# Attention beside a Fourier transform: bursts of six key chunks across the borders of units

## The chip, the cores and the metric

The kernel runs on one core of a Trainium2 chip. The metric is the device time of one execution in microseconds (us). A core has TensorE for matmuls (PE in the rows; PEld are its weight loads), VectorE (DVE), ScalarE (ACT), GpSimd (POOL) and SyncE (SP, which here issues nearly all transfers). Matmuls accumulate in PSUM, eight banks of 128 x 512 fp32; only TensorE, VectorE and ScalarE reach it. Each engine runs its own instructions in order, and waits for other engines at semaphores.

## The reference

Two independent halves, whose outputs stand side by side in `out` (2048 x 2048, fp32).

```
x (2048 x 1024), 32 heads of 32, one key head and one value head for all:
  q = x wq; k = x wk; v = x wv
  p = softmax(q k^T / sqrt(32)) over the 2048 keys, for each head
  out[:, :1024]  = concat_heads(p v) wo
x' (2048 x 1024), Fourier mixing:
  a = x' Dre^T; b = x' Dim^T            (1024 x 1024 matrices)
  out[:, 1024:] = Sre a - Sim b          (2048 x 2048 matrices)
```

## The kernel before, in words

**Two kinds of work share TensorE.** All dense products (the projection to q, the Fourier half, the product with `wo`) are *fills*. A fill is one 128 x 128 by 128 x 512 matmul in fp32r; three of them (high part by high part, high by low, low by high) make one product with more precision. They come in groups, each of which accumulates in one bank `psb` and is then emptied: 32 groups of 24 fills (q), 112 of 12 and 112 of 24 (Fourier, by two schemes of seven products in place of eight), 24 of 24 (`wo`), and at the very end the last eight groups for `wo`. There are two banks `psb` (`ps_b`, line 123).

**Attention runs in steps.** A *unit* is four heads by 512 queries: 32 units, each of 32 steps, 1024 steps in all (the loop over `n` at the end of the kernel). Step `n` belongs to unit `n // 32`. It does these things, in this order:

- `score_step(n + 44)` works 44 steps ahead, on the softmax's row maxima and sums. `scores` makes 128 queries by 1024 keys in a tile `pss` (two matmuls; `ps_s`, line 121, has two such tiles of two banks), VectorE reduces the maximum, and one step later `row_sums` lets ScalarE take the exponentials' sum in the same tile. After a unit's last scores, `lse_1` to `lse_4` combine the sums: small operations on VectorE and ScalarE, and on TensorE one transposition into `psb` (`lse_3`, at n mod 32 = 24). With its own `aside` this stands ahead of the step's scores.
- One function of the list `ends` is run, if there is one.
- `expo` makes the scores once more, transposed (128 keys by two heads of 512 queries, tile `pst`, two matmuls; `ps_t`, line 122, has one such tile), and ScalarE writes the exponentials `p`. Two steps make a *chunk* of 128 keys; a unit has 16 chunks. There are 13 tiles `p` (line 586).
- At n mod 32 = 16 `inverse` loads the unit's reciprocal sums, spread over partitions, to the one tile `rb`.
- At n mod 32 = 0, 12 and 22 comes a *burst*, `pv` (line 686): fp32 matmuls of the values with the waiting chunks `p`, four heads side by side in the array's columns. The three bursts of a unit take 6, 5 and 5 chunks (`CUT`), the third one at step 0 of the next unit. A burst accumulates in a bank `psb`; VectorE copies the first into `ov` and adds the others. After the third, three functions go to `ends`, one for each of the next three steps: GpSimd multiplies `ov` by `rb`, rounds it into `oh`, and takes the rest into `ol`; `store` then sends both to memory over SP.
- `level(n)` deals out fills with `take`, except in a burst step. `goal(n)` is the number of fills due at step `n`, linear in `n`. Up to the next burst, `level` takes in each step the rounded-up share of what is missing to the goal at that burst, so that a stretch of steps between two bursts has its longer steps first.

**`aside`** (line 368) runs ahead of each burst and each transposition. If the open group has had fewer than six of its fills, or has fewer than six left, it takes fills up to that point, so that the other bank `psb` has been emptied, or the group is closed. What it takes is missing from what `level` deals out later.

**What sets the order.** Every engine's instructions are issued in the order in which the program states them (`Ordered`, line 58). Which of a pool's buffers a tile gets is decided when the program is built: a tile takes a buffer whose former tile has been released by its last reader, and waits for that reader on the chip. Loads, splits into high and low parts and stores of the fills are issued ahead of their use by a number of fills (`Line`).

The lines that the change touches are `CUT` and `pv`, `ENDS` and `level`, the burst in the loop over `n`, and the last burst behind it.

Of the kernel before, what the change touches and what calls it, by code (L numbers as in the profile page):

```python
# [8 lines left out]
F32 = mybir.dt.float32  # L9
F32R = mybir.dt.float32r  # L10
# [6 lines left out]
P = 128  # L17
# [3 lines left out]
DH = 32  # L21
W = 512
NG = 8
NQ = 4
NC = 16
# [62 lines left out]
def tile_kernel(ctx: ExitStack, tc, xT, wq, wkv, wo, xbT, wT, cT, out):  # L88
    nc = tc.nc
    te = Ordered(tc, nc.tensor)  # L90
    act = Ordered(tc, nc.scalar)
    dve = Ordered(tc, nc.vector)
    gp = Ordered(tc, nc.gpsimd)
# [3 lines left out]
    def pool(stack, name, bufs, **kw):  # L97
        kw.setdefault("reuse_waits", "tile")
        return stack.enter_context(tc.tile_pool(name=name, bufs=bufs, **kw))
# [4 lines left out]
    oh_d = [dram.tile([NG, P, W], F32, name=f"oh_{b}") for b in range(NQ)]  # L104
    ol_d = [dram.tile([NG, P, W], F32, name=f"ol_{b}") for b in range(NQ)]
# [10 lines left out]
    v = keep.tile([P, NC, DH], F32, name="v")  # L116
# [4 lines left out]
    ps_s = pool(ctx, "ps_s", 2, space=PSUM)  # L121
# [12 lines left out]
    def move(q, to, of):  # L134
        q.dma_start(to.bitcast(F32), of.bitcast(F32))
# [117 lines left out]
    def add(gs):  # L253

        for g in gs:
            i0 = g.at = end[0]
            end[0] += g.n
            if groups and g.set[0] is not groups[-1].set[0]:
                prev["set"] = prev["this"]
                prev["this"] = i0  # L260
            for c, it in enumerate(g.right):
                if it.need is None:
                    it.need = i0 + 3 * c
                    p0 = prev["set"]
                    it.due = min(it.need, p0 + (i0 - p0) * (g.first + c + 1) // (len(g.set) * len(g.right)))
                    RL.items.append(it)
                it.last = i0 + 3 * c + 2
            for c, it in enumerate(g.left):
                if it.need is None:
                    it.need = it.due = i0 + 12 * c  # L270
                    ML.items.append(it)
                it.last = i0 + 12 * c + 11
            for it in g.ys:
                it.due = i0 + g.n
                ylist.append(it)
            groups.append(g)
# [24 lines left out]
    def soon(f):  # L301

        if pos["fill"] <= START:
            f()
        else:
            at(pos["fill"] + BEHIND, f)

    def store(to, of, key=None):
        def go():
            move(sp, to, of)  # L310
            if key:
                ready.add(key)
        soon(go)

    cur = {"at": 0, "bank": None, "group": 0}
    used = [0, 0]

    def bank(name, open_=False):

        b = 1 - cur["bank"] if cur["bank"] is not None else int(used[1] < used[0])  # L320
        cur["at"] += 1
        used[b] = cur["at"]
        if open_:
            cur["bank"] = b
        return ps_b[b].tile([P, W], F32, name=name)
# [16 lines left out]
    def take(n):  # L342
        for _ in range(n):
            if cur["group"] >= len(groups):
                return
            g = groups[cur["group"]]
            j = pos["fill"] - g.at
            if j == 0:
                cur["ps"] = bank("psb", True)
            if j % 3 == 0:  # L350
                RL.force(g.right[j // 3])
            if j % 12 == 0:
                ML.force(g.left[j // 12])
            product(g, cur["ps"], j)
            pos["fill"] += 1
            if j == g.n - 1:
                cur["group"] += 1
                assert all(hasattr(it, "done") for it in g.ys)
                g.post(cur["ps"])
                cur["at"] += 1  # L360
                used[cur["bank"]] = cur["at"]
                cur["bank"] = None
                if g.ys:
                    at(pos["fill"] + 2 * BEHIND, lambda n=len(g.ys): yused.__setitem__(0, yused[0] + n))
            pump()
            run_later()

    def aside():

        if cur["group"] >= len(groups):  # L370
            return
        g = groups[cur["group"]]
        j = pos["fill"] - g.at
        if 0 < j < 6:
            take(6 - j)
        elif j > g.n - 6:
            take(g.n - j)
# [33 lines left out]
    def q_group(b, g, xs):  # L411
        left = [Item([(lambda q=q: wq[g, :, q * 4:(q + 1) * 4, :], 1)]) for q in range(2)]

        def post(ps):
            qh = op.tile([P, W], F32R, name="qh")
            ql = yp.tile([P, W], F32, name="y0").bitcast(F32R)
            if pos["fill"] <= START:
                act.activation(qh, ps, AF.Copy, scale=scale)
            else:
                dve.tensor_scalar_mul(qh, ps, scale)  # L420
            dve.scalar_tensor_tensor(ql, ps, scale, qh.bitcast(F32), op0=ALU.mult, op1=ALU.subtract)
            store(qh_d[b][g], qh)
            store(ql_d[b][g], ql, ("q", b, g))
        return Group(left, xs, post)
# [104 lines left out]
    def wo_set(e):  # L529
        return [Item([(lambda g=g: wo[g * P:(g + 1) * P, e * W:(e + 1) * W], 1)]) for g in range(NG)]  # L530
# [45 lines left out]
    start = [q_group(0, g, sets[0]) for g in range(2)]  # L576
# [12 lines left out]
    onp = pool(ctx, "onp", 1)  # L589

    units = [(b, g) for b in range(NQ) for g in range(NG)]
    SU = 32
    LEAD = 12
    total = SU * len(units)
    qst, nm, lse, pt, ov, rb, pend = ({} for _ in range(7))
    ends = []
# [84 lines left out]
            te.matmul(ps[:, a], kst[:, c * P:(c + 1) * P], qst[u][:, 2 * hp_ + a], start=True, stop=True)  # L681
        act.activation(pt[u, c, hp_], ps, AF.Exp)

    CUT = (0, 6, 11, NC)

    def pv(u, k):

        aside()
        ps = bank("psb")
        for c in range(CUT[k], CUT[k + 1]):  # L690
            for h in range(4):
                te.matmul(ps[h * DH:(h + 1) * DH], v[:, c], pt[u, c, h // 2][:, h % 2], start=c == CUT[k], stop=c == CUT[k + 1] - 1)
        if k == 0:
            ov[u] = onp.tile([P, W], F32, name="ov")
            dve.tensor_copy(ov[u], ps)
        else:
            dve.tensor_add(ov[u], ov[u], ps)
        cur["at"] += 1
        if k == len(CUT) - 2:
            b, g = units[u]  # L700
            hi_ = onp.tile([P, W], F32R, name="oh")
            lo_ = onp.tile([P, W], F32R, name="ol")
            lse["out"] = hi_, lo_

            last = u + 1 == len(units)
            e = dve if last else gp

            def low():
                e.tensor_sub(lo_, ov[u], hi_.bitcast(F32))
                if not last:  # L710
                    store(oh_d[b][g], hi_)
                    store(ol_d[b][g], lo_, ("o", b, g))

            ends.append(lambda: e.tensor_mul(ov[u], ov[u], rb[u]))
            ends.append(lambda: e.tensor_copy(hi_, ov[u]))
            ends.append(low)

    def score_step(s):

        if s < total:  # L720
            u, r = divmod(s, SU)
            if r == SU - 6 and u + 1 < len(units):
                open_unit(u + 1)
        if SU <= s < SU * (len(units) + 1) and s % SU == TURN:
            lse_3((s - SU) // SU)
        if s < total:
            scores(s)
        row_sums(s - 1)
        u, e = divmod(s - SU, SU)
        if 0 <= u < len(units):  # L730
            for f in LSE.get(e, ()):
                f(u)
# [52 lines left out]
    def goal(n):  # L785
        return PRO + (FILL - PRO - LAST - MORE * (total - QUIET)) * n // total + MORE * max(n - QUIET, 0)


    ENDS = [2 * c for c in CUT]

    def level(n):
        r = n % SU
        if r in ENDS:
            return
        more = min(e for e in ENDS if e > r) - r
        left = goal(n + more) - pos["fill"]
        take(left - left * (more - 1) // more)

    for n in range(total):
        u, r = divmod(n, SU)  # L800
        if n == total - 12:
            w1 = wo_set(1)
            add([o_group(NQ - 1, t, e, ws) for e, ws in ((0, w0), (1, w1)) for t in range(4)])
        score_step(n + SU + LEAD)
        if ends:
            ends.pop(0)()
        expo(n)
        if r == 16:
            inverse(u)
        if r in ENDS and n:  # L810
            pv((n - 1) // SU, (ENDS.index(r) - 1) % (len(CUT) - 1))
        level(n)


    last = groups[len(groups) - 8:]
    take(last[0].at - pos["fill"] - 12)
    pv(len(units) - 1, len(CUT) - 2)
    while ends:
        ends.pop(0)()
    hi7, lo7 = lse["out"]  # L820
# [27 lines left out]
    for t, g in enumerate(last[4:]):  # L848
        ps = whole(4 + t)
# [41 lines left out]
```

## Time and profile before

| what | us |
|---|---|
| median of 3 runs (lowest, highest) | 2753.52 (2752.26, 2755.05) |
| the profiled execution | 2752.88 |
| its span, first to last instruction | 2750.8 |
| TensorE busy | 2742.4 |
| ScalarE busy | 2165.2 |
| GpSimd busy | 1596.6 |
| VectorE busy | 1579.5 |

The granted clock of TensorE is 1.000 over the whole span. A row of a timeline gives the start in us from the span's start, the duration, engine, operation, output<-input and the count of instructions merged in the row; in brackets the idle time before it. A row of the groups gives the count, busy us and mean ns of one, then idle time before. A row of the waits gives us in total, times, and the longest. An fp32 matmul stands as two records, an fp32r matmul as one. Every line of the program shows as one and the same line of a helper, so groups are told apart by their tiles' names: `psb<-p,v` are the bursts, `psb<-rh,mh` and its two companions the fills, `pss<-kst,qst` the scores, `pst<-qst,kst` the transposed scores.

### The profile page before, as it was taken

What the parts mean: (1) busy time and instruction counts of PE and PEld (TensorE: products, weight loads), DVE (VectorE), ACT (ScalarE), POOL (GpSimd) and SP (SyncE); (2) the same over time, 40 slices, a digit from 0 to 9 for tenths busy, and PEclk for the clock granted to TensorE, in tenths of its full rate; (3) what the DMA queues carried; (4) which work ended last, traced back from release to release, by engine and by line L of the source; (5) the groups of instructions that cost most, each with busy time, mean ns of one, the idle gap of its engine ahead of it and who ended that gap; (6) DMA issues with size and microseconds to landing.
All of it is one profiled execution on the core that took longest, in us unless ns stands there. A gap on an engine that the chain in (4) does not pass through costs nothing.

```text
span 2750.8 us, 40206 instructions
## 1 busy us (share of the span) xinstructions
PE 2742.4 (100%) x13868; PEld 1928.3 (70%) x13868; DVE 1579.5 (57%) x1798; ACT 2165.2 (79%) x3131; POOL 1596.6 (58%) x1591
## 2 busy tenths in 40 slices
PE   9999999999999999999999999999999999999999
PEld 6876767677676767667676766767676676767667
DVE  5766666666676666555565555556555555555411
ACT  3588888888888878888888888888888888888741
POOL 4845425555436447875556786787887875630110
PEclk9999999999999999999999999999999999999999
DMA  8543335775676556664454675665664753554455
GB/s 272 192 135 122 120 114 178 236 233 184 200 255 201 165 166 188 185 195 131 138 161 146 202 225 158 196 213 166 197 214 151 220 161 116 172 173 139 129 166 177
DMA packets 318720, 487.88 MB, mean 177 GB/s; under 512 B 32890, under 2 KB 98170, under 8 KB 318458
## 3 DMA queue, kind: packets, MB, share of 16 engines
q1 hardware_dynamic: 317364, 483.34, 55.8%
q8 instruction: 109, 1.79, 0.3%
q10 hardware_dynamic: 1152, 1.97, 0.2%
q14 instruction: 95, 0.78, 0.1%
HBM read 364.12 MB, written 119.28 MB: 176 GB/s over the span
## 4 chain that ended last, share of the span: by engine, by line
PE 98%; ACT 1%; DVE 0%; DMA 0%; issue 0%; SPq 0%; ACTq 0%
PE psb L66 62%; PE pss L66 19%; PE pst L66 18%; ACT p L66 0%; ACT pss L66 0%; DMA p<-in_xT_dram 0%; DVE nm L66 0%; DMA u<-y 0%; DVE y L66 0%; SPq L66 0%; DVE qh L66 0%; DVE rl L66 0%; ACT rh L66 0%; DVE p L66 0%; ACT nm L66 0%
## 5 line engine op out<-in xcount | busy, mean ns | idle before, releaser
L66 DVE TENSOR_REDUCE nm<-pss 128x1 f32<-128x1024 f32 x1024 | 1252.6, 1223 | 589.9 <-PE pss L66 589.1
L66 ACT ACTIVATE p<-pst 128x1024 f32<-128x1024 f32 x1026 | 1053.3, 1027 | 456.1 <-PE pst L66 453.5
L66 ACT ACTIVATE pss<-pss,nm 128x1024 f32<-128x1024 f32 x1024 | 1111.3, 1085 | 59.6 <-DVE nm L66 57.8
L66 PE MATMUL psb<-rh,mh 128*128 128x512 f32 x1806 | 710.9, 394 | 1.5 <-ACT rh L66 1.0
L66 PE MATMUL psb<-rl,mh 128*128 128x512 f32 x1806 | 709.4, 393 | 0.6 <-DVE rl L66 0.5
L66 PE MATMUL psb<-rh,ml 128*128 128x512 f32 x1806 | 710.0, 393 | 0.0
L66 PE MATMUL pss<-kst,qst 128*128 128x512 f32 x2048 | 653.7, 400 | 0.1
L66 PE MATMUL pst<-qst,kst 128*128 128x512 f32 x2048 | 649.5, 398 | 1.0 <-ACT p L66 0.7
L66 PEld LDWEIGHTS pss<-kst,qst 128*128 128x128 f32 x2048 | 374.6, 188 | 159.9 <-issue 76.3
L66 PE MATMUL psb<-p,v 128*32 128x512 f32 x4096 | 459.3, 594 | 0.0
L66 POOL TENSOR_TENSOR ml<-m,mh 128x512 fp32r<-128x512 f32 x338 | 437.0, 1293 | 38.0 <-ACT mh L66 26.5
L66 PEld LDWEIGHTS pst<-qst,kst 128*128 128x128 f32 x2048 | 377.4, 188 | 108.1 <-ACT p L66 21.6
L66 PEld LDWEIGHTS psb<-rh,mh 128*128 128x128 f32 x1806 | 338.9, 188 | 86.9 <-issue 2.6
L66 PEld LDWEIGHTS psb<-rl,mh 128*128 128x128 f32 x1806 | 338.9, 188 | 80.9 <-DVE rl L66 1.6
L66 PEld LDWEIGHTS psb<-rh,ml 128*128 128x128 f32 x1806 | 338.9, 188 | 79.5
L66 POOL CAST mh<-m 128x512 fp32r<-128x512 f32 x337 | 207.1, 614 | 212.5 <-PE psb L66 182.4
L66 PEld LDWEIGHTS psb<-p,v 128*32 128x32 f32 x4096 | 123.2, 110 | 283.6 <-issue 275.4
L66 POOL CAST rh<-r 128x512 fp32r<-128x512 f32 x208 | 128.1, 616 | 286.9 <-PE psb L66 202.6
L66 POOL TENSOR_TENSOR m<-m,m 128x512 f32<-128x512 f32 x200 | 258.8, 1294 | 51.7 <-DMA m<-in_xbT_dram 28.8
L66 POOL TENSOR_TENSOR rl<-r,rh 128x512 fp32r<-128x512 f32 x208 | 268.6, 1292 | 3.9
L66 POOL TENSOR_TENSOR ov<-ov,rb 128x512 f32<-128x512 f32 x31 | 40.1, 1294 | 317.3 <-DVE ov L66 313.7
L66 POOL TENSOR_TENSOR r<-r,r 128x512 f32<-128x512 f32 x120 | 155.2, 1293 | 114.0 <-DMA r<-in_wT_dram 88.3
(89 smaller groups left out, 891.3 us busy)
## 6 DMA issues: line engine op xcount, KB each, us to landing
m<-in_cT_dram SPq DMA_DIRECT2D x384, 256.0 KB
r<-s SPq DMA_DIRECT2D x192, 256.0 KB
y<-y SPq DMA_DIRECT2D x128, 256.0 KB
r<-in_wT_dram SPq DMA_DIRECT2D x88, 256.0 KB
m<-in_xbT_dram SPq DMA_DIRECT2D x88, 256.0 KB
y<-u SPq DMA_DIRECT2D x80, 256.0 KB
m<-in_wq_dram SPq DMA_DIRECT2D x64, 256.0 KB
qst<-qh SPq DMA_DIRECT2D x64, 256.0 KB
```

What stands on the lines that cost most here:

```text
L66: return lambda *a, **k: self.tc.keep_in_program_order(f(*a, **k))
```

## The change

The grid of bursts no longer follows the units. A burst comes at every twelfth step, n mod 12 = 10, from n = 10 on, and takes the six chunks that are complete and not yet used, counted through over all units; the first takes five, and the last one behind the loop three. That is 86 bursts in place of 96.

A burst whose chunks belong to two units (`cuts` returns two parts) has two accumulators: the first part goes into a bank `psb` as before, the second into a tile of the pool `ps_s`, of which it uses one bank. Each part is emptied by VectorE: a unit's first part is copied to `ov`, a middle one added to `ov`, and a unit's last part is added to `ov` with the result in a tile `oh`, which takes the name and buffer that the rounded part had. GpSimd's three functions then work on that tile: multiply in place, round into `ol`, and subtract in place. `ov` is not read by GpSimd any more. The functions still run in the three steps behind the burst, which is now at n mod 32 = 2, 6 or 10 of the next unit in turn.

`level` leaves out fills in the new burst steps, and counts up to the next of those, or to the end. Step 0, in which no burst is due, now gets fills.

```diff
@@ -681,39 +681,57 @@
             te.matmul(ps[:, a], kst[:, c * P:(c + 1) * P], qst[u][:, 2 * hp_ + a], start=True, stop=True)
         act.activation(pt[u, c, hp_], ps, AF.Exp)
 
-    CUT = (0, 6, 11, NC)
-
-    def pv(u, k):
-
-        aside()
-        ps = bank("psb")
-        for c in range(CUT[k], CUT[k + 1]):
+    BURST = 6
+    FIRST = 5
+
+    def cuts(n):
+
+        c1 = n // 2
+        c0 = max(c1 - BURST, 0) if c1 < total // 2 else FIRST + (c1 - FIRST - 1) // BURST * BURST
+        parts = []
+        while c0 < c1:
+            u, c = divmod(c0, NC)
+            parts.append((u, c, min(c1 - u * NC, NC)))
+            c0 = u * NC + parts[-1][2]
+        return parts
+
+    def pv(u, c0, c1, own):
+
+        ps = ps_s.tile([P, 2 * W], F32, name="pss")[:, :W] if own else bank("psb")
+        for c in range(c0, c1):
             for h in range(4):
-                te.matmul(ps[h * DH:(h + 1) * DH], v[:, c], pt[u, c, h // 2][:, h % 2], start=c == CUT[k], stop=c == CUT[k + 1] - 1)
-        if k == 0:
+                te.matmul(ps[h * DH:(h + 1) * DH], v[:, c], pt[u, c, h // 2][:, h % 2], start=c == c0, stop=c == c1 - 1)
+        cur["at"] += 1
+        if c0 == 0:
             ov[u] = onp.tile([P, W], F32, name="ov")
             dve.tensor_copy(ov[u], ps)
-        else:
+            return
+        if c1 < NC:
             dve.tensor_add(ov[u], ov[u], ps)
-        cur["at"] += 1
-        if k == len(CUT) - 2:
-            b, g = units[u]
-            hi_ = onp.tile([P, W], F32R, name="oh")
+            return
+        b, g = units[u]
+        if u + 1 == len(units):
+            hi_ = onp.tile([P, W], F32, name="oh").bitcast(F32R)
             lo_ = onp.tile([P, W], F32R, name="ol")
             lse["out"] = hi_, lo_
-
-            last = u + 1 == len(units)
-            e = dve if last else gp
-
-            def low():
-                e.tensor_sub(lo_, ov[u], hi_.bitcast(F32))
-                if not last:
-                    store(oh_d[b][g], hi_)
-                    store(ol_d[b][g], lo_, ("o", b, g))
-
-            ends.append(lambda: e.tensor_mul(ov[u], ov[u], rb[u]))
-            ends.append(lambda: e.tensor_copy(hi_, ov[u]))
-            ends.append(low)
+            dve.tensor_add(ov[u], ov[u], ps)
+            ends.append(lambda: dve.tensor_mul(ov[u], ov[u], rb[u]))
+            ends.append(lambda: dve.tensor_copy(hi_, ov[u]))
+            ends.append(lambda: dve.tensor_sub(lo_, ov[u], hi_.bitcast(F32)))
+            return
+        o = onp.tile([P, W], F32, name="oh")
+        dve.tensor_add(o, ov[u], ps)
+        hi_ = onp.tile([P, W], F32R, name="ol")
+
+        def low():
+            lo_ = o.bitcast(F32R)
+            gp.tensor_sub(lo_, o, hi_.bitcast(F32))
+            store(oh_d[b][g], hi_)
+            store(ol_d[b][g], lo_, ("o", b, g))
+
+        ends.append(lambda: gp.tensor_mul(o, o, rb[u]))
+        ends.append(lambda: gp.tensor_copy(hi_, o))
+        ends.append(low)
 
     def score_step(s):
 
@@ -786,13 +804,13 @@
         return PRO + (FILL - PRO - LAST - MORE * (total - QUIET)) * n // total + MORE * max(n - QUIET, 0)
 
 
-    ENDS = [2 * c for c in CUT]
+    def burst(n):
+        return n % (2 * BURST) == 2 * FIRST
 
     def level(n):
-        r = n % SU
-        if r in ENDS:
+        if burst(n):
             return
-        more = min(e for e in ENDS if e > r) - r
+        more = next(k for k in range(1, 2 * BURST) if burst(n + k) or n + k == total)
         left = goal(n + more) - pos["fill"]
         take(left - left * (more - 1) // more)
 
@@ -807,14 +825,18 @@
         expo(n)
         if r == 16:
             inverse(u)
-        if r in ENDS and n:
-            pv((n - 1) // SU, (ENDS.index(r) - 1) % (len(CUT) - 1))
+        if burst(n):
+            aside()
+            for k, part in enumerate(cuts(n)):
+                pv(*part, k)
         level(n)
 
 
     last = groups[len(groups) - 8:]
     take(last[0].at - pos["fill"] - 12)
-    pv(len(units) - 1, len(CUT) - 2)
+    aside()
+    for part in cuts(total):
+        pv(*part, 0)
     while ends:
         ends.pop(0)()
     hi7, lo7 = lse["out"]
```

## The prediction

> **What bounds the kernel now.** I read the page's busy shares and chain first, then the waits, the groups of instructions, and the timelines of TensorE and ScalarE around a burst and at the end of a stretch between two bursts.
>
> ```profile
> span 2750.8 us, 40206 instructions
> PE 2742.4 (100%) x13868; PEld 1928.3 (70%) x13868; DVE 1579.5 (57%) x1798; ACT 2165.2 (79%) x3131; POOL 1596.6 (58%) x1591
> PE 98%; ACT 1%; DVE 0%; DMA 0%; issue 0%; SPq 0%; ACTq 0%
> ```
>
> TensorE carries the end: 98% of the chain. So the time changes by what a change takes out of TensorE's stream, or puts between its instructions. The waits show how little stands between them, and which engine is nearest:
>
> ```profile
> DVE ov L66 <- PE psb L66: 383.5, 96, 8.6
> POOL ov L66 <- DVE ov L66: 313.7, 30, 40.5
> PEld pst L66 <- ACT p L66: 21.6, 84, 0.8
> PE pst L66 <- ACT p L66: 0.7, 3, 0.3
> PE psb L66 <- DVE y L66: 0.6, 1, 0.6
> ```
>
> (us in total, times, longest.) VectorE waits for TensorE at each of the 96 bursts, GpSimd for VectorE behind 30 of the 31 units that it closes; both are early. The nearest engine is ScalarE: `pst` has one buffer, so the next transposed scores wait for the exponentials `p` of the last step. 84 weight loads waited there.
>
> **Part 1, ten bursts fewer.** TensorE around a burst of five chunks (each fp32 matmul is two records, so 40 of them) and around one of six:
>
> ```profile
> 1020.41 0.40 PE L66 MATMUL psb<-rh,ml 128*128 128x512 f32 x1
> 1020.74 4.50 PE L66 MATMUL psb<-p,v 128*32 128x512 f32 x40
> 1025.17 0.73 PE L66 MATMUL pss<-kst,qst 128*128 128x512 f32 x2
> 1025.74 0.62 PE L66 MATMUL pst<-qst,kst 128*128 128x512 f32 x2
> 1026.20 0.40 PE L66 MATMUL psb<-rh,mh 128*128 128x512 f32 x1
> ...
> 1048.28 0.73 PE L66 MATMUL pst<-qst,kst 128*128 128x512 f32 x2
> 1048.94 5.36 PE L66 MATMUL psb<-p,v 128*32 128x512 f32 x48
> 1054.23 0.73 PE L66 MATMUL pss<-kst,qst 128*128 128x512 f32 x2
> ```
>
> A chunk is 0.86 us (5.36 less 4.50). From the last fill at 1020.41 to the scores at 1025.17 are 4.76 us; five chunks are 4.30, an ordinary spacing 0.23 (the `pst` pair at 1025.74 to the fill at 1026.20 is two of them), so 0.23 is the switch in and out. The pair behind the burst then lasts 0.73, where an undisturbed pair lasts 0.63: 0.10 more. One burst costs 0.33 beside its chunks, whatever their number. All 512 chunks stay; 96 bursts become 86 (5, then 84 of 6, then 3): **-3.3 us**, on the path.
>
> **Part 2, the second parts.** A border falls into 31 bursts. Behind it stand 1, 3 or 5 chunks (11, 10 and 10 times: 91 in all), which accumulate in a `pss` tile. The change of accumulator inside a burst I cost at nothing: the fills change banks at each group of 12 or 24 without a wider spacing than 0.23; no gain, since the burst keeps both its ends; the upper bound is the 0.10 behind a burst, 3 us in all. Each such burst has two evacuations, 117 in place of 96:
>
> ```profile
> L66 DVE TENSOR_TENSOR ov<-ov,psb 128x512 f32<-128x512 f32 x64 | 44.0, 687 | 230.0 <-PE psb L66 230.0
> L66 DVE COPY ov<-psb 128x512 f32<-128x512 f32 x32 | 22.1, 692 | 153.5 <-PE psb L66 153.5
> ```
>
> 21 x 0.69 is 14 us more on VectorE. The first part's add runs while TensorE does the second part's chunks (0.86 or more); the second part's copy stands where the single add stands now, ahead of the next row maxima, so nothing behind it moves. Cover: VectorE's 383.5 us of waiting. Who needs the buffer is shown here (the same burst, all engines):
>
> ```profile
> 1020.72 1.13 ACT L66 ACTIVATE pss<-pss,nm 128x1024 f32<-128x1024 f32 x1
> 1021.72 0.25 ACT L66 ACTIVATION_READ_ACCUMULATOR pss<-pss,nm 128x1 f32 x1
> 1025.30 0.69 DVE L66 TENSOR_TENSOR ov<-ov,psb 128x512 f32<-128x512 f32 x1 [5.02 <-PE psb L66]
> 1025.94 1.22 DVE L66 TENSOR_REDUCE nm<-pss 128x1 f32<-128x1024 f32 x1
> ```
>
> `pss` has two buffers. The one that the second part takes was left by the row sums of the step before, ahead of the burst. The scores behind the burst then need the other, whose row sums end at 1021.97, 3.2 us ahead of them; the copy's buffer is needed one step later, after 1025.99. No wait, if the allocator gives the buffers in the order in which they come free. At worst the scores wait for the copy: 1025.99 and 0.05 in place of 1025.17, 0.87 x 31 = 27 us (a rival). I take nothing.
>
> **Part 3, closing a unit.** The sum goes straight into `oh`, and GpSimd works on that, so `ov` is free for the next unit. GpSimd's three operations per unit and SP's two stores stay in number, kind and queue; they move from steps 1 to 3 of the next unit to 3 to 5, 7 to 9 or 11 to 13. All stand ahead of step 16, where SP reloads `rb`. GpSimd waits for VectorE there today (313.7 us), so the reload finds `rb` read; without that cover the reload would hold up the loads behind it on SP. Nothing, with 0 to 2 us as bounds. The end has 3 chunks behind the loop in place of 5; their 12 fills of cover stay.
>
> **Part 4, the fills move.** This is where I expect the cost. Outside bursts a step is four score matmuls and the fills that `level` deals out; in a burst step there are none but those of `aside`. TensorE and ScalarE at the end of a stretch whose last steps have 5, 4, 4 and 4 fills (step starts are the `pss` rows), with the burst behind 857.92:
>
> ```profile
> 849.60 0.63 PE L66 MATMUL pss<-kst,qst 128*128 128x512 f32 x2
> 851.68 0.63 PE L66 MATMUL pss<-kst,qst 128*128 128x512 f32 x2
> 853.54 0.63 PE L66 MATMUL pss<-kst,qst 128*128 128x512 f32 x2
> 854.01 0.62 PE L66 MATMUL pst<-qst,kst 128*128 128x512 f32 x2
> 855.39 0.63 PE L66 MATMUL pss<-kst,qst 128*128 128x512 f32 x2
> 855.91 0.73 PE L66 MATMUL pst<-qst,kst 128*128 128x512 f32 x2
> 857.40 0.63 PE L66 MATMUL pss<-kst,qst 128*128 128x512 f32 x2
> 857.92 0.73 PE L66 MATMUL pst<-qst,kst 128*128 128x512 f32 x2
> ```
>
> ```profile
> 850.73 1.03 ACT L66 ACTIVATE p<-pst 128x1024 f32<-128x1024 f32 x1
> 852.82 1.03 ACT L66 ACTIVATE p<-pst 128x1024 f32<-128x1024 f32 x1
> 854.83 1.03 ACT L66 ACTIVATE p<-pst 128x1024 f32<-128x1024 f32 x1
> 855.74 1.09 ACT L66 ACTIVATE pss<-pss,nm 128x1024 f32<-128x1024 f32 x1
> 856.82 1.04 ACT L66 ACTIVATE p<-pst 128x1024 f32<-128x1024 f32 x1
> ```
>
> A step of five fills takes 2.08 (849.60 to 851.68), one of four 1.86, so three take 1.63 and two 1.40. ScalarE, where it waits for nothing, goes round in 1.99 (854.83 to 856.82). From the end of the exponentials to the `pst` that overwrites them, 853.85 to 854.01, 0.16 is left after the first short step; after a step of five it is 0.39. After the second it is 0.05, which is the least seen, and TensorE waits. Spare are thus 0.34: the first four-fill step uses 0.23, each further one 0.13 (1.99 less 1.86), one of three 0.36, one of two 0.60; each late pair also lasts 0.10 longer. Two fours at the end of a stretch cost 0.15 (0.05 and 0.10). Three cost 0.31: the step from 855.39 takes 2.01, 0.15 too long, and the burst step's pair comes 0.06 late and lasts 0.10 longer. One costs nothing.
>
> How many there are follows from the planner, not from the trace: its lines stepped through with 404 fills done ahead of step 0 and groups of 24 (32 of them), 12 (112), 24 (136). Runs of short steps at stretches' ends, steps 0 to 979 (later steps have no row scores):
>
> - before, stretches of 11, 9 and 9 steps: 10 of two fours, 4 of three; 10 x 0.15 + 4 x 0.31 = 2.7 us
> - after, all of 11: 8 of two fours (1.2), 9 of three (2.8), 2 of four (0.9), 1 of five (0.6), 2 of five and a three (2.0), and one each of 4-3 (0.35), 3-3 (0.7), 3-2 (0.9), 4-2-2 (1.3): 10.8 us
>
> Four-fill steps go from 41 to 77, and nine of three or two are new. The reason: the transposition of each unit's sums (n mod 32 = 24) takes up to five fills in advance, as does a burst. Today a burst stands two steps ahead of it; then it falls anywhere in a stretch, at worst two steps before the end. **+8.1 us.**
>
> Step 0 has no fills today, as a burst step without a burst. It pays for that once:
>
> ```profile
> 137.50 0.63 PE L66 MATMUL pss<-kst,qst 128*128 128x512 f32 x2
> 137.97 0.62 PE L66 MATMUL pst<-qst,kst 128*128 128x512 f32 x2
> 138.66 0.73 PE L66 MATMUL pss<-kst,qst 128*128 128x512 f32 x2
> 139.71 0.73 PE L66 MATMUL pst<-qst,kst 128*128 128x512 f32 x2 [0.32 <-ACT p L66]
> ```
>
> The scores come 0.2 late (138.66 for 138.44), the `pst` pair 0.6 late and 0.1 longer. Then five fills stand there: **-0.9 us**. Last, ScalarE's small step for the sums:
>
> ```profile
> L66 ACT ACTIVATE nm<-nm 128x32 f32<-128x32 f32 x32 | 7.3, 229 | 0.0
> ```
>
> It falls on n mod 32 = 21, one step ahead of a burst today. In ten units the next burst will be at 26, behind the short steps: 0 to 0.23 each, I take half, **+1.2 us**.
>
> **Sum.** -3.3 + 8.1 - 0.9 + 1.2 = +5.1 us. The profiled execution took 2752.9 us, 0.6 under the runs' median of 2753.5; it would take 2758.0, the median 2758.6.
>
> **Rivals.** (a) *Not slower:* only the ten switches count, because ScalarE's spare is larger than 0.34 where a stretch begins with more fills, or the deep runs recover at the burst. For it: 67 of the 92 stretches today have no short run. Against it: the waits at 855.91 and 857.92. It decides where the waits grow by less than 4.2 us in place of 8.1; time 2749.3 with none, 2751 with a quarter. (b) *The second part's buffer on the path:* the scores behind 31 bursts take the buffer just filled and wait for the copy, 27 us on top of the sum: 2785. The order of release by ScalarE at 1021.97 and VectorE at 1025.99 speaks against it; a ScalarE late by 4 us would turn it. The Trainium skill, TensorEngine Tiling (Array Packing), section PSUM Bottleneck, says that packing speeds up the array but not the emptying of PSUM, so that this copy may become the bottleneck; by that rule (b) would be the case, and the row of VectorE's 383.5 us of waiting does not bear it out. (c) *Fills meet a full bank:* `aside` ends a group just ahead of a burst whose first part takes the other bank, and the next group waits for two evacuations, 1.4 us; at 5 bursts 7 us more, 2766. Against it: TensorE waited for VectorE at a fill once in all today, 0.6 us.
>
> **Chances.** The sum with its bounds (ScalarE's waits from half to one and a half times 8.1): 2754.5 to 2763, 0.61; (a) 0.22; (b) 0.06; (c) 0.11. A measurement of this kernel tells about 0.2% from no change, 5.5 us: 2748.0 to 2759.0. The sum lies just inside. Of its 0.61, 0.33 are within and 0.28 slower; of (a) 0.19 within, 0.03 faster; (b) and most of (c), 0.15, slower. So faster 0.03, within 0.53, slower 0.44. The range takes in (a) from a quarter of the growth and (c): 2750.5 to 2766.
>
> **What would show it.** 3368 `p,v` records into `psb` and 728 into `pss`; 117 VectorE operations for them; 0.33 us per burst unchanged. Waits of `pst` loads for ScalarE well over 84, with steps of 1.99 in place of 1.86 at stretches' ends, most around n mod 32 = 26 and 30. The prediction is wrong if the scores behind crossing bursts start later than about 0.5 us after the last chunk's spacing, if TensorE waits for VectorE or GpSimd at fills, or if the short steps are not slower than 1.86.

## The result

| | kernel before | changed kernel |
|---|---|---|
| median of 20 runs, us | 2752.65 | 2757.40 |
| lowest and highest, us | 2752.16, 2755.05 | 2756.66, 2758.12 |
| span of the profiled execution, us | 2750.8 | 2755.9 |

The change costs 4.75 us: ratio 1.0016, 95% interval 1.0010 to 1.0023. The forecast was +5.1 us and 2758.6. The prediction held that a measurement tells only some 5.5 us from no change; twenty runs of each kernel tell this one.

The page of the changed kernel begins like that of the kernel before; TensorE is still the engine that carries the end.

```profile
span 2755.9 us, 40197 instructions
PE 2747.6 (100%) x13868; PEld 1927.9 (70%) x13868; DVE 1595.5 (58%) x1819; ACT 2160.3 (78%) x3131; POOL 1597.3 (58%) x1591
PE 96%; ACT 2%; DMA 1%; DVE 0%; issue 0%; POOL 0%; SPq 0%; ACTq 0%; POOLq 0%; DVEq 0%
```

TensorE has the same 13868 instructions and five more us. VectorE has 21 more instructions. ScalarE's share of the chain is 2% in place of 1%, both rounded. The waits point the same way (us in total, times, longest):

```profile
POOL oh L66 <- DVE oh L66: 246.0, 24, 46.1
PEld pst L66 <- ACT p L66: 35.8, 126, 0.6
PEld pss L66 <- ACT pss L66: 4.2, 12, 0.7
PE psb L66 <- DVE y L66: 0.9, 2, 0.6
```

Weight loads of `pst` wait for ScalarE 126 times in place of 84. Weight loads for the scores wait 12 times for the row sums to leave `pss`; before it was 4 times and 1.3 us. A fill waits for VectorE twice in place of once.

A measure that needs no judgment on who waits for whom: I took all spacings between the starts of TensorE's matmuls from step 0 to 979, less the usual spacing of each pair of kinds (a fill behind a fill 0.23 us, and so on), with the chunks and the switches of the bursts left out. The sum is 4.9 us before and 13.5 after, 8.6 more (2.6 in both are the switch behind each transposition). Ten bursts fewer at 0.33 are 3.3 less. Together +5.3; the spans differ by 5.1. Only differences between kernels count in this sum: most fills follow one another a little closer than 0.23 us, which pulls every sum down by about 5. The starts that are late by 10 ns or more add up to 9.6 and 18.5 us, 8.9 apart.

This is the changed kernel at the end of a stretch whose last steps have 4, 4, 4, 4, 4 and 3 fills, with the burst behind it (start and duration in us; step starts are the `pss` rows, the fills and most `pst` rows are left out):

```profile
601.39 0.62 PE L66 MATMUL pss<-kst,qst 128*128 128x512 f32 x2
603.24 0.63 PE L66 MATMUL pss<-kst,qst 128*128 128x512 f32 x2
605.26 0.63 PE L66 MATMUL pss<-kst,qst 128*128 128x512 f32 x2
607.26 0.63 PE L66 MATMUL pss<-kst,qst 128*128 128x512 f32 x2
609.28 0.63 PE L66 MATMUL pss<-kst,qst 128*128 128x512 f32 x2
611.06 0.63 PE L66 MATMUL pss<-kst,qst 128*128 128x512 f32 x2
611.79 0.74 PE L66 MATMUL pst<-qst,kst 128*128 128x512 f32 x2
612.69 5.36 PE L66 MATMUL psb<-p,v 128*32 128x512 f32 x48
617.97 0.72 PE L66 MATMUL pss<-kst,qst 128*128 128x512 f32 x2
```

Steps of four fills, 1.86 by themselves, take 2.02, 2.00 and 2.02 us, which is ScalarE's round; the step of three takes 1.78 in place of 1.63, and the `pst` pair of the burst step comes 0.73 behind its scores in place of 0.46. The bursts themselves have their old length: from 611.79 and its late pair to 617.97, 5.36 for the 48 records.

### The profile page after: what moved, and what is told of

The parts are those of the page before. It is cut to its first block, busy times and chain, and to the rows that moved or that the text cites. A ratio compares the mean times of both kernels' runs of the same rounds, so it can differ in the third digit from the quotient of the medians.

```text
span 2755.9 us, 40197 instructions
## 1 busy us (share of the span) xinstructions
PE 2747.6 (100%) x13868; PEld 1927.9 (70%) x13868; DVE 1595.5 (58%) x1819; ACT 2160.3 (78%) x3131; POOL 1597.3 (58%) x1591
## 4 chain that ended last, share of the span: by engine, by line
PE 96%; ACT 2%; DMA 1%; DVE 0%; issue 0%; POOL 0%; SPq 0%; ACTq 0%; POOLq 0%; DVEq 0%
PE psb L66 57%; PE pss L66 21%; PE pst L66 18%; ACT pss L66 1%; ACT p L66 1%; DMA out_dram<-y 0%; DVE nm L66 0%; DVE y L66 0%; DMA r<-s 0%; SPq L66 0%; DMA rb<-r 0%; DMA m<-in_wq_dram 0%; POOL y L66 0%; DMA u<-y 0%; POOL ml L66 0%
## 5 line engine op out<-in xcount | busy, mean ns | idle before, releaser
L66 PE MATMUL psb<-p,v 128*32 128x512 f32 x3368 | 379.2, 595 | 0.0
L66 PEld LDWEIGHTS psb<-p,v 128*32 128x32 f32 x3368 | 100.6, 109 | 231.6 <-issue 223.7
L66 ACT ACTIVATION_READ_ACCUMULATOR pss<-pss,nm 128x1 f32 x1024 | 211.1, 206 | 0.0
```

Of the source, the lines that this page charges most:

```text
L66: return lambda *a, **k: self.tc.keep_in_program_order(f(*a, **k))
```

## The experiments

### The buffer of the second part: read from the trace

Rival (b) needed no run. This is a burst of the changed kernel across a border, five chunks and one, on TensorE and on VectorE:

```profile
945.23 0.63 PE L66 MATMUL pss<-kst,qst 128*128 128x512 f32 x2
947.17 4.50 PE L66 MATMUL psb<-p,v 128*32 128x512 f32 x40
951.49 1.04 PE L66 MATMUL pss<-p,v 128*32 128x512 f32 x8
952.46 0.73 PE L66 MATMUL pss<-kst,qst 128*128 128x512 f32 x2
954.65 0.63 PE L66 MATMUL pss<-kst,qst 128*128 128x512 f32 x2
```

```profile
951.79 0.69 DVE L66 TENSOR_TENSOR oh<-ov,psb 128x512 f32<-128x512 f32 x1 [4.67 <-PE psb L66]
952.60 0.69 DVE L66 COPY ov<-pss 128x512 f32<-128x512 f32 x1
953.23 1.23 DVE L66 TENSOR_REDUCE nm<-pss 128x1 f32<-128x1024 f32 x1
```

The second part starts 4.32 us behind the first: five chunks of 0.86 are 4.30, so the other accumulator costs 0.02 at most. From the first record to the scores are 5.29 us, and 5.28 in the burst above, which has one accumulator. The scores start at 952.46, 0.97 behind the second part's start, before its copy (952.60 to 953.29) has even begun: they have the other buffer. No burst up to step 979 has its scores later than 0.52 us behind the start of its last record, which is the spacing in the kernel before too. TensorE does not wait for the copy.

### Fills dealt out evenly

In the changed kernel:

```diff
-        take(left - left * (more - 1) // more)
+        ahead = pos["fill"] - goal(n)
+        least = 0 if n >= QUIET else 3 if more == 11 and ahead >= 4 else 5
+        take(max(left - left * (more - 1) // more, least))
```

> The changed kernel, in which `level` deals out no step of fewer than five fills (the step right behind a burst may have three where the fills are four or more ahead of their goal; the last 44 steps are as before). Work and bursts stay. My theory (the changed kernel loses its time in runs of short steps, in which TensorE waits for ScalarE): the waits of 10 to 14 us go but for about 2, so 2745 to 2747 us, 10 to 12 below the changed kernel's 2757.4 and 6 to 7 below the kernel before. Rival 1 (the second parts cost about 0.25 us each, as a wait for the buffer or for VectorE, which a stretch's fills do not change): 2755 to 2757. Rival 2 (fills dealt out earlier find their operands not ready): slower than 2757, with waits of TensorE for GpSimd or transfers.

In the kernel before:

```diff
-        take(left - left * (more - 1) // more)
+        least = 5 if n < QUIET else 0
+        take(max(left - left * (more - 1) // more, least))
```

> The kernel before, with no step of fewer than five fills up to the last 44 steps. My theory: it loses its own 2.7 us in runs of short steps, so 2749 to 2750 us, and stays 3 to 4 us above the changed kernel with the same cure, which is the price of ten bursts. Rival 1: no lower than 2752, and the changed kernel with the cure is not below it.

| | us, median | ratio to the kernel before, 95% interval | spacings' excess, us |
|---|---|---|---|
| changed, even fills | 2744.83 | 0.9970 (0.9958 to 0.9981) | 0.7 |
| before, even fills | 2750.25 | 0.9990 (0.9981 to 0.9999) | 1.3 |

The same stretch with even fills has a step every 2.08 to 2.09 us up to the burst:

```profile
604.65 0.63 PE L66 MATMUL pss<-kst,qst 128*128 128x512 f32 x2
606.74 0.63 PE L66 MATMUL pss<-kst,qst 128*128 128x512 f32 x2
608.82 0.63 PE L66 MATMUL pss<-kst,qst 128*128 128x512 f32 x2
610.91 0.63 PE L66 MATMUL pss<-kst,qst 128*128 128x512 f32 x2
611.37 0.62 PE L66 MATMUL pst<-qst,kst 128*128 128x512 f32 x2
611.92 5.36 PE L66 MATMUL psb<-p,v 128*32 128x512 f32 x48
617.21 0.73 PE L66 MATMUL pss<-kst,qst 128*128 128x512 f32 x2
```

The changed kernel gains 12.6 us by it, a little over what I expected, and the kernel before 2.4. No step was made longer by operands that came late. So the loss of the changed kernel is how its fills were dealt out, not its bursts and not its second parts. With even fills on both sides the change is worth 5.4 us, where I expected 3 to 4: 3.3 for the switches and 0.6 for the waits that are left (the kernel before still has a step 0 without fills). The remaining 1.5 us are smaller than the scatter of the kernel before with even fills (2748.49 to 2752.19), and I cannot place them; between the two profiled executions the gap is 4.7 us (2744.59 and 2749.30). The changed kernel with even fills is the fastest version here, 0.30% below the kernel before.

### ScalarE's round made shorter

In both kernels the row sums read and write only half of the columns; what follows from the sums is then computed from half of the keys:

```diff
-        act.activation(ps, ps, AF.Exp, bias=..., accum_out=...)
+        act.activation(ps[:, :W], ps[:, :W], AF.Exp, bias=..., accum_out=...)
```

> The changed kernel, in which ScalarE's row sums read and write 512 of the 1024 columns; so the sums miss half of the keys. TensorE's stream and the planner's fills are the same. ScalarE's round falls from 1.99 to about 1.56 us, under the 1.86 and 1.63 of steps with four and three fills. My theory: the waits at stretches' ends vanish, 2744 to 2747 us. Rival 1 (second parts on the path): 2754 to 2757, since ScalarE has nothing to do with it.

> The kernel before with the same halved row sums (the sums miss half of the keys). My theory: 2747.5 to 2749.5 us, its own waits of 3 to 5 us gone; the changed kernel with halved row sums is then 3.3 us faster (2.5 to 4.5), the ten switches of bursts alone. Rival 1: the changed kernel stays slower than this one.

Measured: 2746.01 us for the changed kernel (0.9975 of the kernel before, 0.9964 to 0.9985) and 2748.04 for the kernel before (0.9982, 0.9973 to 0.9991). TensorE's stream and the planner's short steps are untouched, and 11.4 us of the changed kernel's time are gone with ScalarE's shorter round: the waits are for ScalarE. The order of the two kernels turns round. But the gap is 2.0 us, not 3.3, and below what I had set. The excess of the spacings says why: 1.7 us in the changed kernel, 0.4 in the other. A remainder stays at steps of three and two fills, as here, with a step of three at the end:

```profile
1326.44 0.63 PE L66 MATMUL pss<-kst,qst 128*128 128x512 f32 x2
1326.91 0.63 PE L66 MATMUL pst<-qst,kst 128*128 128x512 f32 x2
...
1328.08 0.63 PE L66 MATMUL pss<-kst,qst 128*128 128x512 f32 x2
1328.65 0.74 PE L66 MATMUL pst<-qst,kst 128*128 128x512 f32 x2
```

```profile
1327.57 1.03 ACT L66 ACTIVATE p<-pst 128x1024 f32<-128x1024 f32 x1 [0.17 <-PE pst L66]
1328.49 0.66 ACT L66 ACTIVATE pss<-pss,nm 128x512 f32<-128x512 f32 x1
```

ScalarE was idle for 0.17 us and took up the exponentials 0.66 behind the start of their scores; they last 1.03, and 0.05 later the next pair may start. From pair to pair that is 1.74 whatever else ScalarE does. With one `pst` buffer no step can be shorter, and one of three fills (1.63) still waits 0.1.

### The price of a burst by itself

The kernel before with halved row sums, as above, and six bursts per unit:

```diff
-    CUT = (0, 6, 11, NC)
+    CUT = (0, 3, 6, 9, 11, 13, NC)
```

> The kernel before with halved row sums (the sums miss half of the keys) and six bursts per unit, of 3, 3, 3, 2, 2 and 3 chunks, in place of three: 192 bursts in place of 96, the same 512 chunks. It prices a burst by itself. My theory (0.33 us for each burst, whatever its length): 31.6 us above the kernel before with halved row sums, 28 to 35. Rival (the price lies in the chunks, or is hidden): within 5 us of it.

Measured: 2776.46 us, 28.4 above the kernel before with halved row sums, 0.30 for each of 96 bursts; at the lower edge of what I expected. A burst of two chunks:

```profile
1007.38 0.39 PE L66 MATMUL psb<-rh,ml 128*128 128x512 f32 x1
1007.70 1.92 PE L66 MATMUL psb<-p,v 128*32 128x512 f32 x16
1009.55 0.73 PE L66 MATMUL pss<-kst,qst 128*128 128x512 f32 x2
1010.12 0.62 PE L66 MATMUL pst<-qst,kst 128*128 128x512 f32 x2
```

From the fill to the scores are 2.17 us. Two chunks are 1.72 and an ordinary spacing 0.23, which leaves 0.22, and the pair behind lasts 0.73 in place of 0.63: again 0.32 to 0.33, the same as around five or six chunks. The price hangs on the number of bursts and not on their length. The Trainium skill, TensorEngine Tiling (Array Packing), section Key Properties, says that changing the tiling mode drains TensorE; this agrees with a price per switch, for which the page has no figure. The missing 3 us are not in the bursts. Between the two profiled executions, from which these rows are, the gap is 30.3 us (2779.37 and 2749.07), 0.32 for each burst; the first lies 2.9 above the median of its kernel and the second 1.0, so 1.9 of the 3 are scatter between executions. The remaining 1.3 us I cannot place.

### Both parts in a bank

```diff
-        ps = ps_s.tile([P, 2 * W], F32, name="pss")[:, :W] if own else bank("psb")
+        ps = bank("psb")
```

> The changed kernel, in which the second part of a crossing burst goes into a bank `psb` like the first, in place of a row scores' tile. Mostly that is the bank that the first part has just filled, so TensorE waits in the burst until VectorE has emptied it: from the rows of a burst about 0.9 us each (0.13 to the add's start, 0.69 for it, 0.05 behind it), 31 times. My theory: 25 to 30 us above the changed kernel, 2782 to 2788. Rival (the wait is used up by ScalarE's lateness, which the burst then need not pay): under 15 us above it.

Measured: 2781.32 us, 23.9 above the changed kernel, just under the range. The waits of this kernel:

```profile
PEld psb L66 <- DVE oh L66: 38.8, 22, 1.8
PE psb L66 <- DVE oh L66: 18.8, 22, 0.9
```

TensorE waited in 22 bursts of the 31 and not in all: 23.9 us are 1.09 each. I had the price per wait nearly right (0.9) and the number wrong. Where `aside` has just closed a group, both banks are free, and the second part gets the other one: of the 30 crossing bursts up to step 979, nine do not wait so, and they are the nine that stand at the border of a group by the planner's rules. So the row scores' tile is worth 24 us: had the change kept to the banks, it would have cost 29 us in place of 5. The Trainium skill says in TensorEngine Tiling (Array Packing), section PSUM Bottleneck, that packing does not speed up the emptying of PSUM. The same 0.69 us of emptying a bank is found in both kernels here; it costs TensorE nothing behind a buffer that is free, and 1.09 us a time where the array needs the buffer next.

### Where the short steps come from

In both kernels the transposition of a unit's sums no longer calls for fills in advance; the bursts still do:

```diff
     def lse_3(u):
-        aside()
```

> The changed kernel without `aside` ahead of the transposition of a unit's sums; the bursts keep theirs. It tests where the short steps come from. By the planner's rules steps of three and two fills vanish and four-fill steps go from 77 to 50, mostly one or two in a run. My theory (the transposition's fills in advance make the deep runs): about 8 us of waits go, 2748 to 2751 us; where the transposition now comes early in a group, it can wait for VectorE to empty the other bank, up to 0.7 us in about a quarter of 32 units, up to 5 us back. Rival (the deep runs come from the bursts' own grid): 2755 to 2757.

> The kernel before without the same `aside`. By the planner's rules its four-fill steps go from 41 to 27. My theory: about 2 us of waits go, up to 5 us may come back as waits for the other bank: 2750 to 2755 us, so that the changed kernel without it is 0 to 5 us faster in place of 4.7 slower. Rival: the difference of the two stays at 4 to 5 us.

Measured: 2752.47 us for the changed kernel (0.9999 of the kernel before, 0.9990 to 1.0008) and 2750.00 for the kernel before (0.9990, 0.9981 to 0.9999). The changed kernel wins 4.9 us, 1.5 to 4.5 less than I expected, and stays 2.5 behind the kernel before treated alike, where I expected it level or up to 5 faster; the kernel before is at the lower edge of its range. The excess of its spacings falls from 13.5 to 8.5. Of the 8.5, 3.1 us are new and stand at six transpositions, as here:

```profile
1320.72 0.39 PE L66 MATMUL psb<-rh,mh 128*128 128x512 f32 x1
1320.92 0.69 DVE L66 COPY qh<-psb 128x512 f32<-128x512 f32 x1 [0.16 <-PE psb L66]
...
1321.66 0.10 PEld L66 LDWEIGHTS psb<-ident,nm 128*48 128x48 f32 x1 [0.98 <-DVE qh L66]
1321.67 0.29 PE L66 MATMUL psb<-ident,nm 128*48 128x128 f32 x1 [0.56 <-DVE qh L66]
```

A new group has had two fills, VectorE is emptying the other bank, and the transposition waits for it; that is what `aside` prevents. What it prevents costs 3.1 us here; what it causes, some 8: 6.1 in the runs of short steps behind it, and 1.7 at the transpositions themselves, where the fills that it takes close a group and the next ones find a full bank (both counted from late starts). The kernel before had none of the six waits, since its transpositions meet the groups at other places. So the transposition's fills in advance make about 8 of the changed kernel's 13.5 us; 5.4 stay without them, where the kernel before keeps 2.2.

## Why the prediction was right

**The sum.** +5.1 us forecast, +4.75 measured; +4.8 between the profiled executions, +5.1 between their spans. The parts can mostly be told apart. Three hold by themselves, and the fourth holds as a sum, in part by luck:

- *Ten bursts fewer, -3.3.* 86 bursts are there, and a burst costs the same 0.33 around two, three, five or six chunks. As a difference between whole kernels the price came out as 0.30 (medians) and 0.32 (profiled executions) per burst.
- *Second parts, nothing.* 3368 and 728 records, 117 operations on VectorE. Neither the other accumulator nor the copy shows in TensorE's stream. The change's own risk, rival (b), did not come; its price is 24 us where the buffer is chosen otherwise.
- *Closing a unit later, nothing.* GpSimd still waits for VectorE's last add (24 times, 246.0 us), and TensorE for neither.
- *Short steps, +8.1, step 0, -0.9, ScalarE's small step, +1.2.* Together +8.4; the spacings have 8.6, or 8.9 by late starts alone. The counts that the planner's rules gave are those of the trace: in all steps from 0 to 974 the fills between the `pst` pair and the next scores are as many as stepped through ahead of time. Halved row sums and evenly dealt fills, which take away one side of the wait each, both remove 11 to 13 us.

Split by the steps in which the late starts stand, the 8.9 are these. Step 0 gives its -0.9. The runs of short steps and the small step together, which cannot be told apart, give +7.3, where the two terms have +9.3. The rest was in no term of the sum: +0.5 at transpositions (below), and +2.0 at steps of five fills or more outside such runs. So two misses of about 2 us cancel. Six of the eight places outside such runs in the changed kernel (the kernel before has two) look like this one, some rows left out:

```profile
813.73 1.29 DVE L66 TENSOR_TENSOR y<-y,psb 128x512 f32<-128x512 f32 x2 [0.40 <-PE psb L66]
814.93 2.58 DVE L66 TENSOR_REDUCE nm<-pss 128x1 f32<-128x1024 f32 x2
816.24 1.09 ACT L66 ACTIVATE pss<-pss,nm 128x1024 f32<-128x1024 f32 x1 [0.51 <-DVE nm L66]
817.35 1.01 ACT L66 ACTIVATE p<-pst 128x1024 f32<-128x1024 f32 x1
817.70 0.63 PE L66 MATMUL pss<-kst,qst 128*128 128x512 f32 x2
818.42 0.73 PE L66 MATMUL pst<-qst,kst 128*128 128x512 f32 x2
```

VectorE empties a bank ahead of the row maxima, ScalarE waits 0.51 for the maximum, and the `pst` pair comes 0.72 behind its scores in place of 0.46, in a step of five fills. With halved row sums no late start is left at such steps.

**What was not right in it.** The working had one limit for ScalarE, its round of 1.99. Two more limits showed up. With two fills in a step the *scores* wait too, since the row sums of two steps ago still hold their buffer:

```profile
762.54 0.19 ACT L66 ACTIVATION_READ_ACCUMULATOR pss<-pss,nm 128x1 f32 x1
762.78 0.73 PE L66 MATMUL pss<-kst,qst 128*128 128x512 f32 x2 [0.27 <-ACT pss L66]
```

And there is the chain from pair to pair of 1.74 us. Neither changes the sum by more than about 1 us here. Rival (c), fills that meet a full bank, came twice in place of once, 0.5 us more, and not at the bursts but at transpositions. The prediction had waits of TensorE for VectorE at fills among its signs of being wrong; this one is there, too small to turn the account.

**The reason named for the short steps** holds in part. I named both kinds of fills in advance, and put the growth down to those of the transposition. Without these the excess is still 8.5 us in the changed kernel against 2.2 in the kernel before: 3.1 at transpositions, and most of the rest in stretches that a burst's own `aside` has shortened. This last is worked out and not measured: stepped through with neither `aside`, the planner's rules leave one run of short steps in the changed kernel and none in the kernel before.

Two slips in the working do not touch the sum: by the planner's rules 69 of the 92 stretches have no short step, and not 67, and the chances for within and slower add up from their parts to 0.54 and 0.43.

## What to carry to other kernels

When the busiest engine shows 100% busy, waits hide in the length of its steps: compare the spacing of like instructions, and look for the engine whose round is next to the shortest step (here 1.99 against 1.86 us). A change that moves work from fixed places into a grid is costed by how evenly the rest is then dealt out, which a planner's own rules tell ahead of time; here that was worth more than the saving that the grid brought, and three lines in the planner took the loss away and left the saving. Where work may be taken in advance to avoid a wait, count also the shorter steps that it leaves behind.

## What the runs showed that I had not expected

ScalarE's rows grow where it runs without a gap: over the stretch shown above, six exponentials in a row are recorded as longer and longer, while their starts stay 1.99 us apart (the rows of the row sums between them are left out):

```profile
602.68 1.02 ACT L66 ACTIVATE p<-pst 128x1024 f32<-128x1024 f32 x1
...
606.66 1.06 ACT L66 ACTIVATE p<-pst 128x1024 f32<-128x1024 f32 x1
...
612.64 1.11 ACT L66 ACTIVATE p<-pst 128x1024 f32<-128x1024 f32 x1
```

(602.68 to 612.64 is five rounds of 1.99.) So the engine's rate is read from starts, and not from durations. The longer rows do delay whoever waits for their end: the `pst` pair that follows comes up to 0.09 us later than the first row's length would let it. Why they grow, these runs do not settle.
